# Loads of late weight operands and output weights moved from SyncE's to ScalarE's queue in a gated mix of two linear attentions

## The chip, the cores and the metric

The kernel runs on one core of a Trainium2 chip. A core has five engines with instruction streams of their own: TensorE (PE, matmuls and transposes), VectorE (DVE), ScalarE (ACT), GpSimd (POOL) and SyncE (SP, which here issues transfers only). They wait for each other on semaphores. Transfers (DMAs) are issued by an engine and carried out by 16 DMA engines. The metric is the time of one execution on the device in microseconds (us).

## The reference

Tokens x (2048 x 576) go through two linear attentions of 32 heads with 18 columns each, A and B, whose outputs are mixed by a gate:

```python
def _A_ref(x, wqkv, wo):
    qkv = (lambda x, *d: x.transpose(*d))((x @ wqkv).reshape(B, S, 3, H, Dh), 2, 0, 3, 1, 4)
    q, k, v = qkv[0], qkv[1], qkv[2]
    phi = lambda t: jnp.where(t > 0, t + 1, jnp.exp(t)) + 1e-6
    pq, pk = phi(q), phi(k)
    kv = jnp.einsum("bhsd,bhse->bhde", pk, v)
    z = jnp.einsum("bhsd->bhd", pk)
    num = jnp.einsum("bhqd,bhde->bhqe", pq, kv)
    den = jnp.einsum("bhqd,bhd->bhq", pq, z)[..., None] + 1e-6
    ...  @ wo

def _B_ref(x, wqkv, w_phi, wo):
    ...
    pq = jnp.einsum("bhsd,hdf->bhsf", q, w_phi)
    pk = jnp.einsum("bhsd,hdf->bhsf", k, w_phi)
    phi_q = jnp.concatenate([_softmax(pq, axis=-1), _softmax(-pq, axis=-1)], axis=-1)
    phi_k = jnp.concatenate([_softmax(pk, axis=-1), _softmax(-pk, axis=-1)], axis=-1)
    ...

g = _sigmoid((x * gate_w).sum(-1, keepdims=True))
return g * a + (1 - g) * b
```

## The kernel before

**Tiles and passes.** The 2048 tokens are 16 tiles of 128, worked on in pairs. Every projection is a Strassen product of seven smaller products, whose operands are split in a high and a low part. The weight operands of the seven products lie in `op` tiles (a pool of 11 buffers, 128 x 2304 values each) and `tail` tiles. Three passes follow each other. A's pass makes A's keys and values and adds up A's `kv`; it also forms the x operands and stores them in DRAM (`x0x` to `x3x`, `s0x` to `s2x`). B's pass does the same for B, with the x operands loaded again by `x_fetch`, one pair ahead, into `xu`, `xp`, `x` and `xv`. The query pass computes both queries of a pair, both numerators and denominators, and the output rows.

**Work beside the passes.** In the passes, generators are stepped forward between products. In A's pass `prep_b` and `prep_q1` fold the weights of B. In B's pass `both` (L1003) runs `prep_wo`, then `prep_out` (L918), which multiplies A's `kv` into A's output weight, six column blocks one after the other, in `op` tiles, and stores the rows in DRAM as `MA_d` (named `mad` in the profile); then `prep_q2`, which makes the query weights' operands. At its end `prep_out` copies rows 378 to 570 of `MA_d` into free places of `WO_d` (`wod`), the other half of the output weights, DRAM to DRAM. Of the seven weight operands, four stay in `op` tiles as they are made; operands 7, 4 and 3, the late ones, are written to DRAM (`stage`, the tile `st`, 256 x 1 x 576 in each store; `wb` for B, `wq` for the queries) and come back at the end of the pass by `load_ops` (L619): for B at L914, for the queries at L1033.

**The start of the query pass.** When the query pass begins to run ahead by a pair, `x_fetch` loads the next pair's x operands and `load_out` (L1036) the output weights: four `op` tiles and a tail, three of them from `WO_d` and the rest from `MA_d`, with two small pieces of two rows each. The output matmuls `bk<-op,at` need all of them. The fold of B's `kv` runs there too: ScalarE copies it to `z_b` and `kb`, and PE goes on from there. `late` is a tile that holds queries' features, which PE transposes (`tr<-ident,late`).

**What sets the order.** All engine calls are first recorded as `Op`s of a `Plan`. `weigh` (L201) gives each a cost; that of a DMA is 450 or 740 ns on SP and 60 ns on another engine, with a lag of 5 us. `order` (L234) works back from PE's sequence to the time at which each instruction is due. `run` (L268) then simulates the engines and picks, among those that are ready, the one that is due first; a DMA there goes through one server for all, at 370 bytes a ns. `plan.first` adds a dependence for this planning alone: `load_out`'s loads are planned behind the x loads (`x["dma"]`). `emit` (L343) issues the whole list in the order found, so that in the profile every instruction has line L351. On the chip an engine runs its list in order, and PE too. Semaphores are set for real dependences and for buffers; besides, the DMAs take eight completion semaphores in turn, so that an issue also waits for the landing of the DMA eight issues earlier, whichever engine issued it.

```python
            op.cost = 60 if eng != "SP" else 740 if op.dma < 20000 else 450
            ...
            if op.dma:
                dma = max(s + 1000, dma) + op.dma / 370
                end = dma + 750
```

Of the kernel before, what the change touches and what calls it, by code (L numbers as in the profile page):

```python
# [144 lines left out]
class Plan:  # L145
# [55 lines left out]
    def weigh(self, op, eng, name, out, ins, args, kw):  # L201
        n = max([math.prod(v.shape[1:]) for v in (*ins, out) if isinstance(v, View)])
        psum = any(v.tile.psum for v in (*ins, out) if isinstance(v, View))
        wide = any(v.idx.strides[-1] == 0 for v in ins)
        if name == "dma_start":
            op.dma = math.prod((out if isinstance(out, View) else ins[0]).shape) * 4
            op.cost = 60 if eng != "SP" else 740 if op.dma < 20000 else 450
            op.lag = 5000
        elif eng == "ACT":
            op.cost += 190 + .87 * n  # L210
        elif eng == "POOL":
            tt = name == "tensor_tensor"
            op.cost += (200 + 1.7 * n if wide else 150 + 2.2 * n) if tt else 80 + .85 * n
            op.lock = tt
        elif eng == "DVE":
            fast = name in ("tensor_scalar", "tensor_copy", "memset") and not psum
            op.cost += 120 + 5 * n if name == "reciprocal" else 120 + .6 * n if fast else 80 + 1.04 * n if psum else 75 + 1.03 * n
            op.lag = 85
            op.lock = not psum and name in ("tensor_tensor", "tensor_scalar", "scalar_tensor_tensor")
        else:  # L220
            m = out.shape[0]
            op.lag = self.PE_OUT
            if ins[0].dtype() == F32R and name == "matmul":
                op.cost += 5 + .441 * n if m > 64 else 3 + .221 * n
                op.mode = m <= 64
            elif name == "transpose":
                op.cost += 108
            else:
                n = math.prod(out.shape[1:])
                half = m <= 64 or ins[0].shape[0] <= 64  # L230
                op.cost += 6 + .82 * n if m <= 64 else max(112, 1.75 * n)
                op.mode = half
# [35 lines left out]
    def run(self, tags):  # L268
        ops = self.ops
        for op in ops:  # L270
            op.left, op.est = len(op.deps), 0
        free = {e: 800 for e in ("PE", "ACT", "DVE", "POOL", "SP")}
        ready = {e: [] for e in free}
        slots = {tag: [0] * ts[0].bufs for tag, ts in tags.items()}
        pend = {tag: list(ts) for tag, ts in tags.items()}
        started, last, left = set(), {}, {t: t.ops for ts in tags.values() for t in ts}
        for op in ops:
            if not op.left:
                ready[op.eng].append(op)
        lock, dma, mode = 0, 0, False  # L280
        out = []
        SL = {"PE": 120, "ACT": 250, "DVE": 250, "POOL": 100, "SP": 50}
        while len(out) < len(ops):
            best = None
            for e, ops_e in ready.items():
                cand = []
                for op in ops_e:
                    s = max(free[e], op.est)
                    taken = {}
                    for t in op.tiles:  # L290
                        if t not in started:
                            free_at = sorted(slots[t.tag])
                            k = taken[t.tag] = taken.get(t.tag, -1) + 1
                            if pend[t.tag].index(t) >= len(free_at):
                                s = None
                                break
                            s = max(s, free_at[k])
                    if s is None:
                        continue
                    if op.lock:  # L300
                        s = max(s, lock - (220 if e == "POOL" else 30))
                    cand.append((s, op, 110 if e == "PE" and op.mode != mode else 0))
                if not cand:
                    continue
                first = min(s for s, _, _ in cand)
                due, _, s, op = min((op.due + 2 * turn, op.i, s + turn, op) for s, op, turn in cand if s <= first + SL[e])
                if best is None or s < best[0]:
                    best = (s, e, op)
            s, e, op = best
            ready[e].remove(op)  # L310
            for t in op.tiles:
                if t not in started:
                    started.add(t)
                    pend[t.tag].remove(t)
                    slots[t.tag].remove(min(slots[t.tag]))
            end = s + op.cost
            free[e] = end
            if op.dma:
                dma = max(s + 1000, dma) + op.dma / 370
                end = dma + 750  # L320
            elif e == "PE":
                mode = op.mode
            if op.lock:
                lock = end
            if not op.dma:
                end += op.lag
            op.key = s
            out.append(op)
            for t in op.tiles:
                left[t] -= 1  # L330
                last[t] = max(last.get(t, 0), end + self.SEM)
                if not left[t]:
                    slots[t.tag].append(last[t])
            for i in op.succ:
                o = ops[i]
                o.left -= 1
                o.est = max(o.est, free[e] if o.eng == e and not op.dma else end + self.SEM)
                if not o.left:
                    ready[o.eng].append(o)
        self.span = max(free.values())  # L340
        return out
# [14 lines left out]
def tile_gated_mix(ctx, tc, xT, wAk, wAv, wBv, wAq, wkT, wqT, phi, woA, woB, out):  # L356
# [12 lines left out]
    def r(ap):  # L369
        return ap.bitcast(F32)  # L370
# [248 lines left out]
    def load_ops(W, Wd, x):  # L619
        for op in (7, 4, 3):  # L620
            W[op] = op_tile()
            plan.first = ()
            SP.dma_start(r(W[op]), Wd[op])

    def folds(src, K, ph, raw, ahead):

# [291 lines left out]
    def prep_out():  # L918
# [27 lines left out]
        for c in range(6):  # L946
            wo, nxt = nxt, load(c + 1) if c < 5 else None
            here = [(a, 2 * c + a) for a in range(2 if c < 5 else 1)]
            if c % 2 == 0:
                t = op_tile()  # L950
            k, rows = 2 * (c % 2), 64 * len(here)
            pm = pq_tile()
            with plan.piece():
                for hf in range(2):
                    for a, gr in here:
                        h = slice(64 * a, 64 * a + 54)
                        PE.matmul(pm[64 * a:64 * a + 64, hf, :HB], KA[h, 54 * gr:54 * gr + 64], wo[h, HB * hf:HB * hf + HB],
                                  start=True, stop=True, skip_group_check=True)
            hv, lv = [t[:rows, k + s].rearrange("p (a c) -> p a c", a=2) for s in range(2)]
            A.activation(hv, pm[:rows, :, :HB], AF.Copy)  # L960
            V.tensor_tensor(lv, pm[:rows, :, :HB], r(hv), op=ALU.subtract)
            if c < 4:
                if c % 2:
                    dst = MA_d[108 * (c - 1):108 * (c + 1)].rearrange("(c a q) s n -> a q c s n", c=2, a=2)
                    for a in range(2):
                        SP.dma_start(dst[a], r(t[64 * a:64 * a + 54]).rearrange("p (c s) n -> p c s n", c=2))
            else:
                for a, gr in here:
                    n = min(54, D - 54 * gr)
                    SP.dma_start(MA_d[54 * gr:54 * gr + n], r(t[64 * a:64 * a + n, k:k + 2]))  # L970
            yield
        for a in range(2):
            SP.dma_start(WO_d[64 * a + 54:64 * a + 64, 0:5], MA_d[378:478].rearrange("(k a q) s n -> a q k s n", a=2, q=10)[a])
        SP.dma_start(WO_d[36:, 5], MA_d[478:570])
# [28 lines left out]
    def both():  # L1003
        yield from prep_wo()
        yield from prep_out()
        yield from prep_q2()

    prep = both()
    a_done, pend = pend, []
# [26 lines left out]
    def load_out(x):  # L1036
        for k in range(4):
# [2 lines left out]
            to = r(t).rearrange("p (i s) n -> p i s n", i=2)  # L1040
            plan.first = x["dma"]
            if k < 3:
                SP.dma_start(to, WO_d[:, 2 * k:2 * k + 2])
            else:
                SP.dma_start(to[:126], MA_d[:252].rearrange("(g p) s n -> p g s n", g=2))
                SP.dma_start(to[126:], MA_d[570:574].rearrange("(g p) s n -> p g s n", g=2))
        t = tail_tile()
        WOt.append(t)
        plan.first = x["dma"]
        SP.dma_start(r(t[:126]), MA_d[252:378])  # L1050
        SP.dma_start(r(t[126:]), MA_d[574:])

    WOt = []

# [297 lines left out]
```

## Time and profile before

| what | us |
|---|---|
| median of 3 runs | 574.15 (575.48, 571.35, 574.15) |
| the profiled execution | 575.83 |
| its span on the core | 574.1, at a mean granted PE clock of 0.993 |

The profile is of one execution, taken by the hardware profiler. Its names are those of tiles, out<-in, without buffer numbers: `op<-wod` is the load of an `op` tile from `WO_d`, `pq<-op,xu` a matmul of a weight operand with `xu` into `pq`. SPq and ACTq are the parts of SP and ACT that issue transfers. A matmul of 288 columns is listed with about 297 ns in the groups, but matmuls overlap, so that work on PE is read from one row's start to the next one's. The granted clock is a share of PE's full speed. The DMA share is the busy share of the 16 DMA engines. The late operands for B leave SP from 124.33 on, at the end of A's pass, and those for the queries up to 276.83, at the end of B's; the start of the query pass is what happens from 300 to 340.

### The profile page before, as it was taken

The numbers are of one execution on the slowest core, as the hardware profiler recorded it, in microseconds if no ns is written. First come the engines' busy times: TensorE is split into PE (matmuls) and PEld (weight loads), VectorE is DVE, ScalarE is ACT, GpSimd is POOL, SyncE is SP. The second block draws the span as 40 slices with busy tenths as digits, with TensorE's granted clock in tenths as the row PEclk, the third lists the DMA queues.
The fourth block names the chain that finished last, engine by engine and source line by source line (L and its number), as shares of the span: only waits on it lengthen the run. The fifth ranks groups of instructions, "written<-read, shape, count | busy, mean of one in ns | idle before, by whom it ended". The sixth has DMA issues, their size and how long they took to land.

```text
span 574.1 us, 11726 instructions
## 1 busy us (share of the span) xinstructions
PE 555.1 (97%) x4584; PEld 529.5 (92%) x4584; DVE 422.8 (74%) x665; ACT 286.4 (50%) x602; POOL 252.4 (44%) x226
## 2 busy tenths in 40 slices
PE   8999999999999998999899799999999999999997
PEld 8999999999999888999898789898998989999897
DVE  7773479723799877999879878959679595987910
ACT  6766687556644433443345455345354354435431
POOL 5683798642954312543228645124242241523200
PEclk9999999999999999999999799999999999999999
DMA  8768567999795666667949522132232313200011
GB/s 305 253 212 280 182 244 274 319 322 385 259 396 169 201 209 209 210 216 217 384 126 324 214 84 74 41 117 72 77 94 67 104 66 104 76 2 22 22 42 41
DMA packets 40209, 100.73 MB, mean 175 GB/s; under 512 B 4282, under 2 KB 7610, under 8 KB 38618
## 3 DMA queue, kind: packets, MB, share of 16 engines
q1 hardware_dynamic: 40154, 99.99, 50.7%
q8 instruction: 36, 0.59, 0.4%
q14 instruction: 19, 0.16, 0.1%
HBM read 64.15 MB, written 36.70 MB: 176 GB/s over the span
## 4 chain that ended last, share of the span: by engine, by line
PE 73%; DVE 11%; DMA 8%; POOL 3%; issue 2%; ACT 2%; SPq 1%; POOLq 0%; ACTq 0%; DVEq 0%
PE pq L351 30%; PE bk L351 23%; PE tr L351 19%; DMA xu<-x0x 3%; DVE row L351 2%; DVE at L351 2%; DMA x<-x3x 2%; DVE ss L351 1%; DMA wq<-st 1%; DMA wb<-st 1%; DVE mm L351 1%; DMA uw<-wqT 1%; DVE vo L351 1%; DVE dd L351 1%; DVE uw L351 1%
## 5 line engine op out<-in xcount | busy, mean ns | idle before, releaser
L351 PE MATMUL pq<-op,x 128*128 128x288 f32 (+1 forms) x636 | 102.4, 297 | 0.0
L351 PEld LDWEIGHTS pq<-op,x 128*128 128x128 f32 x636 | 90.1, 188 | 0.7 <-issue 0.4
L351 PE MATMUL bk<-op,vo 128*128 128x288 f32 x480 | 71.0, 297 | 0.0
L351 PE MATMUL pq<-tail,x 128*128 128x288 f32 (+1 forms) x308 | 66.7, 300 | 2.0 <-DMA x<-x3x 2.0
L351 PEld LDWEIGHTS bk<-op,vo 128*128 128x128 f32 x480 | 65.8, 188 | 0.2 <-DVE vo L351 0.2
L351 PE MATMUL pq<-op,xp 128*128 128x288 f32 (+1 forms) x336 | 54.2, 298 | 0.0
L351 PEld LDWEIGHTS pq<-tail,x 128*128 128x128 f32 x308 | 49.0, 188 | 3.4 <-issue 2.9
L351 PE MATMUL bk<-op,at 128*128 128x288 f32 x288 | 52.1, 305 | 0.0
L351 POOL TENSOR_TENSOR row<-row,z_a 128x576 f32<-128x576 f32 x16 | 22.7, 1420 | 65.3 <-issue 35.6
L351 PEld LDWEIGHTS pq<-op,xp 128*128 128x128 f32 x336 | 47.7, 188 | 0.2
L351 ACT ACTIVATE row<-bk 128x288 f32<-128x288 f32 x38 | 15.6, 410 | 64.3 <-PE bk L351 64.3
L351 ACT ACTIVATE row<-row,epsc 128x576 f32<-128x576 f32 x54 | 41.9, 776 | 10.1 <-DVE row L351 9.0
L351 DVE TENSOR_TENSOR row<-row,pq 128x576 f32<-128x576 f32 (+1 forms) x30 | 22.5, 751 | 32.0 <-ACT row L351 16.0
L351 POOL TENSOR_TENSOR row<-row,den 128x378 f32<-128x378 f32 (+1 forms) x32 | 24.6, 787 | 48.5 <-DVE den L351 40.0
L351 ACT ACTIVATE row<-tr 128x288 f32<-128x288 f32 (+1 forms) x74 | 29.8, 407 | 30.0 <-PE tr L351 29.6
L351 DVE TENSOR_REDUCE ss<-uw 128x64 f32<-128x1152 f32 x23 | 30.9, 1349 | 16.8 <-ACT uw L351 16.1
L351 PEld LDWEIGHTS bk<-op,at 128*128 128x128 f32 x288 | 42.5, 192 | 0.4 <-issue 0.4
L351 ACT ACTIVATE uw<-uw 128x1152 f32<-128x1152 f32 x23 | 26.7, 1165 | 28.5 <-DVE uw L351 18.7
L351 POOL TENSOR_TENSOR x<-at,x 128x384 fp32r<-128x384 f32 (+2 forms) x36 | 31.3, 877 | 21.0 <-ACT x L351 11.9
L351 DVE TENSOR_TENSOR at<-at 128x256 f32<-128x256 f32 (+1 forms) x40 | 31.2, 817 | 7.4 <-DMA at<-xT 7.0
L351 ACT ACTIVATE uT<-tr 118x512 f32<-118x512 f32 (+1 forms) x48 | 25.9, 559 | 20.9 <-PE tr L351 20.8
L351 PE MATMUL tr<-op,xv 128*128 128x288 f32 (+1 forms) x204 | 34.0, 303 | 0.0
(184 smaller groups left out, 1264.6 us busy)
## 6 DMA issues: line engine op xcount, KB each, us to landing
xp<-s0x SPq DMA_DIRECT2D x14, 512.0 KB
at<-xT SPq DMA_DIRECT2D x20, 320.0 KB
x<-x1x SPq DMA_DIRECT2D x14, 384.0 KB
x<-s2x SPq DMA_DIRECT2D x14, 384.0 KB
s0x<-xp SPq DMA_DIRECT2D x8, 512.0 KB
out<-row SPq DMA_DIRECT2D x14, 288.0 KB
xu<-x0x SPq DMA_DIRECT2D x14, 256.0 KB
x<-s1x SPq DMA_DIRECT2D x14, 256.0 KB
```

Source lines behind the costliest of these rows:

```text
L351: fn(*[a.real() if isinstance(a, View) else a for a in args], **{k: v.real() if isinstance(v, View) else v for k, v in kw.items()})
```

## The change

Three things are edited. `load_ops` and `load_out` issue their loads on ScalarE (`A.dma_start`) instead of SP, 13 DMAs in all. The copies from `MA_d` into `WO_d` leave `prep_out` for a new generator, `join_out`, which `both` runs after `prep_q2`, that is, at the end of B's pass as the code is written. And the planner changes its model: a DMA on another engine than SP costs 350 ns instead of 60, and there is a server of transfers for each of the two queues, at 370 bytes a ns or 185 while the other is busy.

```diff
-            op.cost = 60 if eng != "SP" else 740 if op.dma < 20000 else 450
+            op.cost = 350 if eng != "SP" else 740 if op.dma < 20000 else 450
@@ run
-        lock, dma, mode = 0, 0, False
+        lock, dma, mode = 0, {"SP": 0, "ACT": 0}, False
@@
-                dma = max(s + 1000, dma) + op.dma / 370
-                end = dma + 750
+                dma[e] = max(s + 1000, dma[e]) + op.dma / (370 if max(dma.values()) <= s + 1000 or dma[e] > s + 1000 else 185)
+                end = dma[e] + 750
@@ load_ops
             W[op] = op_tile()
-            plan.first = ()
-            SP.dma_start(r(W[op]), Wd[op])
+            A.dma_start(r(W[op]), Wd[op])
@@ prep_out
             yield
+
+    def join_out():
         for a in range(2):
             SP.dma_start(WO_d[64 * a + 54:64 * a + 64, 0:5], MA_d[378:478].rearrange("(k a q) s n -> a q k s n", a=2, q=10)[a])
         SP.dma_start(WO_d[36:, 5], MA_d[478:570])
@@ both
         yield from prep_q2()
+        yield from join_out()
@@ load_out
             if k < 3:
-                SP.dma_start(to, WO_d[:, 2 * k:2 * k + 2])
+                A.dma_start(to, WO_d[:, 2 * k:2 * k + 2])
             else:
-                SP.dma_start(to[:126], MA_d[:252].rearrange("(g p) s n -> p g s n", g=2))
-                SP.dma_start(to[126:], MA_d[570:574].rearrange("(g p) s n -> p g s n", g=2))
+                A.dma_start(to[:126], MA_d[:252].rearrange("(g p) s n -> p g s n", g=2))
+                A.dma_start(to[126:], MA_d[570:574].rearrange("(g p) s n -> p g s n", g=2))
...
-        SP.dma_start(r(t[:126]), MA_d[252:378])
-        SP.dma_start(r(t[126:]), MA_d[574:])
+        A.dma_start(r(t[:126]), MA_d[252:378])
+        A.dma_start(r(t[126:]), MA_d[574:])
```

Since the planner lays out the whole program, the order of the engines' lists changes where due times and costs changed. SP's list in the middle of B's pass, where A's output rows are stored (`mad<-op`) and copied (`wod<-mad`) between the loads of the next pair's x operands:

```order
-L351 DMA x_2690<-s1x_991 128x512
+L351 DMA x_2691<-s1x_991 128x512
 L351 DMA wod<-mad 10x5x1152 x2
+L351 DMA mad<-op 36x1152
 L351 DMA xv<-x2x_1023 128x512
-L351 DMA x_2729<-x3x_1060 128x256
-L351 DMA mad<-op 36x1152
-L351 DMA x_2769<-s2x_1077 128x768
+L351 DMA x_2732<-x3x_1060 128x256
+L351 DMA x_2770<-s2x_1077 128x768
 L351 DMA wod<-mad 92x1152
```

The copies stand in the same places in both. The last store of A's rows, 36x1152, moved ahead of the loads of `xv` and x3x.

SP's list at the end of B's pass, with the late query operands (`op<-wq`) and the store of the last of them (`wq<-st`):

```order
 L351 DMA xu<-x0x_155 128x512
-L351 DMA op<-wq_2875 128x2304
-L351 DMA wq_3111<-st 256x1x576
-L351 DMA op<-wq_2980 128x2304
 L351 DMA x_3399<-x1x_165 128x768
-L351 DMA xp<-s0x_1841 128x1024
-L351 DMA op<-wq_3111 128x2304
-L351 DMA x_3479<-s1x_1853 128x512
+L351 DMA xp<-s0x_1820 128x1024
+L351 DMA x_3479<-s1x_1864 128x512
```

The three loads are gone from SP, and the store stands further up in its list.

ScalarE's list at the start of the query pass, where it copies B's folded `kv` from PSUM (`z_b<-bk`, `kb<-bk`):

```order
 L351 ACTIVATE z_b<-bk 128x3x2x54 x2
+L351 DMA op<-mad 126x2x1152
 L351 ACTIVATE z_b<-bk 128x2x2x54 x2
 L351 ACTIVATE z_b<-bk 128x2x36
+L351 DMA tail<-mad 126x1152
+L351 DMA op<-wod 128x2304
 L351 ACTIVATE kb<-bk 108x8x54
 L351 ACTIVATE kb<-bk 108x2x54
 L351 ACTIVATE kb<-bk 72x36
```

Three of the seven loads of the output weights now stand between these copies; the other four come behind them.

PE's list at the same place (`x_3660` is an x operand of the pair in work, `xu` one of the next pair):

```order
 L351 MATMUL bk<-op,xp 128x288 x12
-L351 MATMUL bk<-op,x_3660 128x288 x9
-L351 MATMUL tr<-ident,late 118x128 x8
-L351 MATMUL bk<-op,x_3660 128x288 x3
-L351 MATMUL bk<-op,xv 128x288 x2
+L351 MATMUL bk<-op,x_3660 128x288 x6
+L351 MATMUL pq<-op,xu 128x288
+L351 MATMUL bk<-op,x_3660 128x288 x2
+L351 MATMUL tr<-ident,late 118x128 x8
```

The first matmul on `xu` moved up, ahead of work that stood before it.

PE's list a little further on, where the first output matmuls (`bk<-op,at`, `bk<-tail,at`) stand; `x_3746` is an x operand of the pair in work:

```order
-L351 MATMUL pq<-op,xu 128x288 x12
-L351 MATMUL bk<-op,at 128x288 x6
-L351 MATMUL bk<-tail,at 128x288 x3
-L351 MATMUL pq<-op,x_3746 128x288 x2
-L351 MATMUL tr<-ident,late 118x128 x8
-L351 MATMUL pq<-op,x_3746 128x288 x4
...
+L351 MATMUL pq<-op,xu 128x288 x11
+L351 MATMUL tr<-ident,late 118x128 x8
+L351 MATMUL bk<-op,at 128x288 x6
+L351 MATMUL bk<-tail,at 128x288 x2
```

Eight transposes moved ahead of the output matmuls, and six matmuls on `x_3746` moved behind this place.

## The prediction, on record before the run

> **What bounds the kernel now.** I read the page first: which engine is full, and what ends the chain.
>
> ```profile
> PE 555.1 (97%) x4584; PEld 529.5 (92%) x4584; DVE 422.8 (74%) x665; ACT 286.4 (50%) x602; POOL 252.4 (44%) x226
> PEclk9999999999999999999999799999999999999999
> q1 hardware_dynamic: 40154, 99.99, 50.7%
> PE 73%; DVE 11%; DMA 8%; POOL 3%; issue 2%; ACT 2%; SPq 1%; POOLq 0%; ACTq 0%; DVEq 0%
> ```
>
> TensorE (PE) is busy 97% of the span, so the matmuls set the time and a change of the transfers can win only PE's idle time and the time lost at a low clock. The clock is below full in one slice of 40 only. All data goes through one queue, q1. The chain of work that ended last has 8% of the span in transfers. Next, therefore, PE's waits by what ended them (total us, times, longest):
>
> ```profile
> PE pq L351 <- DMA xu<-x0x: 3.9, 1, 3.9
> PE tr L351 <- ACT uw L351: 2.3, 1, 2.3
> PE pq L351 <- DMA x<-x3x: 2.0, 1, 2.0
> PE pq L351 <- DMA uw<-wqT: 0.9, 1, 0.9
> ```
>
> These are single waits. In PE's timeline (start, busy time, idle time and releaser in brackets) they stand at three places that the change touches, A's last output rows (219.7), the end of B's pass (287.1) and the start of the query pass (322.0):
>
> ```profile
> 219.70 1.87 PE L351 MATMUL tr<-op,xp 128*128 128x288 f32 x12 [2.34 <-ACT uw L351]
> 287.09 0.50 PE L351 MATMUL pq<-tail,x 128*128 128x288 f32 x2 [1.97 <-DMA x<-x3x]
> 309.56 1.36 PE L351 MATMUL bk<-op,x 128*128 128x288 f32 x9
> 317.72 0.42 PE L351 MATMUL pq<-tail,x 128*128 128x288 f32 x2
> 322.04 3.25 PE L351 MATMUL pq<-op,xu 128*128 128x288 f32 x12 [3.89 <-DMA xu<-x0x]
> 325.08 1.65 PE L351 MATMUL bk<-op,at 128*128 128x288 f32 x6
> 327.24 0.43 PE L351 MATMUL pq<-op,x 128*128 128x288 f32 x2
> 327.51 1.03 PE L351 MATMUL tr<-ident,late 128*118 128x128 f32 x8
> 329.51 0.95 PE L351 MATMUL pq<-op,x 128*128 128x288 f32 x6
> 333.50 0.82 PE L351 MATMUL pq<-op,xp 128*128 128x288 f32 x5
> 365.54 0.96 PE L351 MATMUL bk<-op,at 128*128 128x288 f32 x6
> ```
>
> What each cost in clock is in the table by stretch (from:to, length, busy of PE, weight load, VectorE (DVE), ScalarE (ACT) and GpSimd (POOL), clock, DMA share, GB/s):
>
> ```profile
> 124.00:128.00 4.00, 3.08 (x25) 2.87 (x24) 0.76 (x1) 1.28 (x3) 1.61 (x2) 1.00 1.06 407
> 217.00:220.00 3.00, 0.66 (x5) 0.42 (x4) 0.62 (x1) 2.33 (x4) 1.42 (x1) 1.00 0.40 135
> 284.00:288.00 4.00, 2.03 (x16) 1.82 (x15) 3.83 (x6) 0.82 (x2) 0.13 (x1) 1.00 0.75 259
> 304.00:322.00 18.00, 12.99 (x93) 11.66 (x93) 17.38 (x30) 11.14 (x28) 15.25 (x16) 0.96 1.00 333
> 322.00:326.00 4.00, 3.96 (x16) 3.96 (x17) 4.00 (x7) 0.00 (x0) 3.24 (x4) 0.50 0.41 141
> 326.00:328.00 2.00, 2.00 (x14) 2.00 (x13) 1.90 (x5) 0.00 (x0) 0.82 (x2) 0.69 0.40 131
> ```
>
> The waits of 2.34 and 1.97 left the clock at 1.00. That of 3.89 was followed by 0.50 for four microseconds and 0.69 for two: 4 x 0.50 + 2 x 0.31 = 2.6 us of full-clock work lost. The start of the query pass so loses 3.9 + 2.6 = 6.5 us, of which the transfers are the cause, at a DMA share of 1.00 from 304 to 322. The chain gives the transfers themselves (start, time to landing):
>
> ```profile
> 214.55 2.99 DMA mad<-op
> 278.19 8.76 DMA x<-x3x
> 307.09 14.90 DMA xu<-x0x
> 121.82 5.35 DMA uw<-wqT
> 251.68 3.61 DMA wq<-st
> ```
>
> and the list of transfers their sizes, by the number of such transfers and KB of each:
>
> ```profile
> op<-wq SPq DMA_DIRECT2D x3, 1152.0 KB
> x<-x3x SPq DMA_DIRECT2D x14, 128.0 KB
> xu<-x0x SPq DMA_DIRECT2D x14, 256.0 KB
> ```
>
> **The change part by part.** The sum is made against the profiled execution, 575.83 us, which is 1.68 above the median of 574.15.
>
> *A's last output rows.* The words say that the copies into WO_d move to the end of B's pass; the order shows them where they were, so that part costs and brings nothing (both ends zero, unless a queue moves around them). What moves is the last store of A's rows, ahead of two x loads.
>
> ```profile
> 212.83 1.67 SPq L351 DMA_DIRECT2D x<-x3x  x1
> 276.83 0.32 SPq L351 DMA_DIRECT2D op<-wq  x1
> 300.24 0.42 SPq L351 DMA_DIRECT2D op<-mad  x1
> 302.35 1.32 SPq L351 DMA_DIRECT2D op<-wod  x3
> 217.61 0.68 ACT L351 ACTIVATE op<-row 128x576 fp32r<-128x576 f32 x1 [7.35 <-DMA mad<-op]
> 301.53 0.75 ACT L351 ACTIVATE z_b<-bk 128x324 f32<-128x324 f32 x2
> 304.62 0.76 ACT L351 ACTIVATE kb<-bk 108x432 f32<-108x432 f32 x3 [0.62 <-PE bk L351]
> ```
>
> The store was issued at 214.55 and landed 2.99 later, 217.54, and ScalarE, which had waited 7.35 for the buffer that the store reads, went on at 217.61; PE then waited 2.34 for ScalarE's next result. Issued ahead of the x loads it goes out at 212.3 at the earliest, so ScalarE is freed up to 2.2 us sooner. If the store shares the engines with the copies issued at 210.57 it gains about 1. I take the middle, **-1.6** (-1.0 to -2.2). Next late there is VectorE, 0.62 busy of 3 us, so nothing takes the wait's place.
>
> *Late weight operands.* Of the six loads the three of B's pass are issued by ScalarE near 125, where it is 1.28 us busy of 4; they wait there for the landing of earlier transfers, and what is queued behind them on ScalarE is wanted by nobody for microseconds: 0. The third load at the end of B's pass went out at 276.83 on SP, 1152 KB, and x<-x3x behind it took 8.76 us for 128 KB and landed at 286.95, when PE had waited since 285.1. It now leaves from ScalarE, and earlier, since the store that it reads moved ahead too. By the nearest row of a transfer that is not held up, 3.61 for wq<-st, x3x lands at 281.8, 3.3 us before it is asked for. The wait of 1.97 can go whole; but VectorE is 3.83 busy of 4 there, so part can come back as a wait for it: **-1.7** (0 to -2.0).
>
> *Output weights.* The seven loads fill the engines from 304 on, and xu, issued at 307.09 behind all of them in one queue, landed at 321.99. As the queue takes them in order, the output weights were in by then too. Three things happen to them now.
>
> First, ScalarE issues them after its second z_b, at 301.53 + 0.75 = 302.3, 2.0 us after SP did (300.24). Second, xu no longer stands behind them. It still cannot be issued before 307.09, which a matmul's end sets. When it lands the trace does not show: 2.99 is the shortest such transfer in the chain, 14.90 what it took in one queue; I take 5.35, that of uw<-wqT, which ran into saturated engines (share 1.06 in 124 to 128): 307.09 + 5.35 = 312.4. Third, PE's first matmul on xu moves ahead of other work. It comes after six of the nine matmuls of the row at 309.56, so at 309.56 + 0.9 = 310.5, where before PE had 318.14 - 310.5 = 7.65 us of work left ahead of it. PE waits 312.4 - 310.5 = 1.9, less than the 2.34 that left the clock alone. Then come the 7.65 us, to 320.1, the remaining matmuls on xu at full clock, 3.25 / 2 = 1.6, and the eight transposes that now stand ahead of the output matmul, 0.8 of the 1.03: 322.5.
>
> There PE asks for all output weights, bk<-op,at. They end 2.0 us later than at 322.0 for the late start, and later by xu's 256 KB, which at 333 GB/s is 0.7: 324.7 (322 if the start costs nothing, 326.4 if the x loads behind xu pass as well). PE waits 2.2. After it: 0.96 for the six (the full-clock row at 365.54), 0.5 for the tail, 1.1 for what is left up to the row at 329.51, about half of the 2.3 us between 327.24 and there, since the eight transposes are gone from it (six matmuls on x_3746 now stand further back, but PE still has to do them): 327.3. Before it was 329.5: **-2.2** (-6.5 if neither wait appears). That both waits stay under the 2.34 is my choice; should the clock fall, the 2.2 is gone.
>
> By the Trainium skill, DMA: Bandwidth & Descriptors, "Queues, rings and completion order", an engine alternates between the queues that have work, packet by packet; the 256 KB would then go at half of 333 GB/s, an estimate of 1.5 us, xu would land little after 308.6, and the first wait would go, 1.9 more than in the sum above. No row here shows two queues at work.
>
> *ScalarE's price.* SP's rows give 0.3 to 0.44 us for one issue. Two of the seven stand ahead of kb<-bk, at 304.62, which PE waits for; ScalarE had 0.62 us free there, so 2 x 0.44 - 0.62 = **+0.3** (0.1 to 1.0). SP's later x loads still wait for the same transfers to land, but the first, xp, comes to PE only at 333.50.
>
> Sum: -1.6 - 1.7 - 2.2 + 0.3 = **-5.2**: 570.6 on the profiled execution, 569.0 as a median.
>
> **The rivals.** *Slower: xu gets no faster, and PE asks for it sooner.* Both queues end on the same 16 engines, full at 1.00 from 304 to 322, with 333 GB/s for all. If packets are served about in the order of issue, xu still takes 14.9, and now 7.65 us of PE work that ran before it stand behind it: +7.7 at the query start, with the clock as low as before, and 7.7 - 1.6 - 1.7 + 0.3 = +4.7: median 578.9. It decides from a landing 10.2 us after the issue on (322.0 - 4.7 - 307.1). For it: the order of PE did move, and one queue is all the trace shows. Against it: uw<-wqT took 5.35 under a full load, though in the same queue.
>
> *The stall only changes its name.* The bytes are the same, and what PE waits for at 322 becomes the output weights, later by their start and with the clock down again: the third term is 0, 575.83 - 3.0 = 572.8, median 571.1. For it: 333 GB/s through the whole stretch, and DVE at 17.38 of 18. The Trainium skill, DMA: Bandwidth & Descriptors, "Issuing engines are not separate DMA queues", speaks for it: transfers share the same 16 engines whoever starts them, and a second issuer saves issue time alone. The share of 1.00 agrees.
>
> *All of it goes.* xu lands before 310.5, the weights by 322.5: -2.2 - 2.0 - 6.5 + 0.1 = -10.6, median 563.5. Against it: the later start of the weights.
>
> **How the numbers follow.** Forecast 0.45 (own range 566.5 to 571.5), the changed name 0.2, slower 0.2 (574 to 584), all of it 0.15. About 1%, 5.7 us, is what a measurement of this kernel can tell from no change. Faster than 568.4: four tenths of the forecast (0.18), all of it (0.15), a little of the changed name (0.03), 0.36. Slower than 579.9: a little under half of the slower case and 0.03 for what I haven't seen, 0.12. The range 563.5 to 578 leaves out half of each end case.
>
> **What would show it.** Right: two queues with data; ScalarE's op<-row near 216 and no 2.34 behind it; no wait for x3x at 285; xu landing some 5 us after its issue, and PE waiting for op<-wod or op<-mad near 322 with the clock at 1.00. Wrong: xu at 10 us or more after its issue with a PE wait near 311 and a clock of 0.50 behind it; a wait for kb of over 1 us near 305; or the copies to WO_d standing elsewhere than now.

## The result, and the profile after

The changed kernel takes 581.78 us as a median of 6 runs (579.95 to 587.91), against 574.82 for the kernel before on the same chips (6 runs, 571.35 to 581.13): 1.0132 times as long, with a 95% interval of 1.0092 to 1.0171. It is slower, where the prediction was 569.0 with a range of 563.5 to 578. The profiled execution took 579.95 us, with a span of 578.2 against 574.1.

PE's waits and the queues in the profile after, from the table of waits (total us, times, longest) and the page:

```profile
PE pq L351 <- DMA xu<-x0x: 5.6, 1, 5.6
PE pq L351 <- DMA uw<-wqT: 4.5, 2, 3.9
...
PE tr L351 <- ACT uw L351: 1.3, 1, 1.3
```

```profile
q1 hardware_dynamic: 38442, 87.60, 44.4%
q10 hardware_dynamic: 1712, 12.39, 5.6%
```

The wait for x3x is gone and that for ScalarE's `uw` is down from 2.3 to 1.3. But xu now costs 5.6 instead of 3.9, and the `uw<-wqT` loads at the end of A's pass (pieces of B's query weight, 320 KB or less), 0.9 before, cost 4.5. The 13 loads do run in a queue of their own, q10. PE's timeline after, at the two places that lost:

```profile
126.86 1.35 PE L351 MATMUL pq<-at,uw 126*128 126x126 f32 x10 [0.64 <-DMA uw<-wqT]
...
135.87 2.01 PE L351 MATMUL pq<-at,uw 126*128 126x126 f32 x10 [3.88 <-DMA uw<-wqT]
...
318.34 0.58 PE L351 MATMUL pq<-op,xu 128*128 128x288 f32 x1 [5.60 <-DMA xu<-x0x]
...
327.91 1.62 PE L351 MATMUL pq<-op,xu 128*128 128x288 f32 x11
...
330.17 1.04 PE L351 MATMUL bk<-op,at 128*128 128x288 f32 x6
```

`bk<-op,at` has no wait in brackets: the output weights, which the prediction made the second wait, were in. The chain of work after gives the two transfers (start, time to landing), and the table by stretch what the clock did behind them (the eighth number is the clock):

```profile
124.09 11.65 DMA uw<-wqT
...
309.26 8.94 DMA xu<-x0x
```

```profile
132.00:136.00 4.00, 0.13 (x1) 0.16 (x2) 0.68 (x1) 0.72 (x2) 1.26 (x1) 1.00 1.05 359
136.00:140.00 4.00, 4.00 (x21) 4.00 (x22) 0.00 (x0) 1.17 (x3) 0.00 (x0) 0.57 0.99 383
...
318.00:322.00 4.00, 3.66 (x16) 3.67 (x17) 0.00 (x0) 1.19 (x2) 0.23 (x1) 0.50 0.90 372
322.00:326.00 4.00, 4.00 (x26) 3.95 (x25) 2.26 (x6) 3.32 (x8) 1.48 (x2) 0.74 0.19 66
```

Both long waits were followed by a clock of about a half.

All kernels of this case have the same 4584 matmuls on PE, so one can read how far a run lags behind another by comparing the starts of the matmul with the same number. The table takes four stretches, named by the time in the profile of before, and gives how much each profiled execution gained or lost in it against that of before:

| us lost (+) or won (-) | end of A's pass (129.9 to 153.5) | A's last rows (214.8 to 226.2) | end of B's pass (261.1 to 298.9) | query start (298.9 to 346.0) | at the last matmuls |
|---|---|---|---|---|---|
| the changed kernel | +4.9 | -1.1 | -2.2 | +2.2 | +4.1 |
| e1, before's order, 13 loads on ScalarE | +7.5 | +1.8 | +1.7 | -3.6 | +7.6 |
| e2, the new order, 13 loads on SP | +5.4 | -1.2 | -2.2 | +7.0 | +9.7 |
| e3, late operands only | +4.4 | -1.4 | -2.2 | -1.1 | -0.4 |
| e4, output weights only | -0.2 | +3.5 | -1.6 | +1.3 | +3.5 |
| e5, before's order, output weights on ScalarE | 0.0 | +2.4 | -2.0 | -0.7 | -0.5 |
| e6, e5 and the queries' operands | +0.3 | +2.6 | +4.5 | -4.5 | +1.5 |
| e9, one server, B's operands on SP | -0.1 | +2.4 | +2.5 | -5.4 | +1.3 |
| e10, before's order, B's operands on ScalarE | +6.1 | +4.3 | -1.8 | +0.1 | +9.3 |
| e11, one server, output weights on ScalarE | +0.5 | +1.7 | -2.0 | -5.1 | -5.4 |
| e12, e11 and the last store on ScalarE | 0.0 | -2.6 | -2.0 | -5.1 | -9.0 |
| e13, the change, B's operands on SP | -0.2 | +3.5 | +2.7 | +0.7 | +6.3 |

What is left of a row's sum came up at other places. The table shows the noise too: e4, e5, e10 and e11 have before's lists on every engine at A's last rows, and lost 1.7 to 4.3 us there against the one execution of before that was profiled; and with the third `op<-wq` still on SP they won 1.6 to 2.0 at the end of B's pass. So that execution of before was lucky at the first place, by some 2 to 4 us, and unlucky at the second, by about 2.

### The profile page after: what moved, and what is told of

It reads as the page before. It is cut to its first block, busy times and chain, and to the rows that moved or that the text cites. A ratio compares the mean times of both kernels' runs of the same rounds, so it can differ in the third digit from the quotient of the medians.

```text
span 578.2 us, 11728 instructions
## 1 busy us (share of the span) xinstructions
PE 557.1 (96%) x4584; PEld 531.6 (92%) x4584; DVE 419.7 (73%) x665; ACT 287.8 (50%) x602; POOL 252.7 (44%) x226
## 4 chain that ended last, share of the span: by engine, by line
PE 78%; DVE 11%; DMA 6%; POOL 2%; issue 1%; ACT 1%; POOLq 0%; ACTq 0%; DVEq 0%
PE pq L351 33%; PE tr L351 23%; PE bk L351 22%; DMA uw<-wqT 2%; DVE row L351 2%; DMA wq<-st 2%; DVE ss L351 2%; DVE den L351 2%; DMA xu<-x0x 2%; DVE dd L351 1%; DVE mm L351 1%; DVE rs L351 1%; DVE uw L351 1%; DMA x<-x3x 1%; POOL late L351 1%
## 5 line engine op out<-in xcount | busy, mean ns | idle before, releaser
L351 DVE TENSOR_TENSOR vo<-row,pq 128x540 f32<-128x540 f32 (+1 forms) x56 | 22.8, 449 | 17.9 <-ACT row L351 15.0
```

The costliest lines, as they stand in the source:

```text
L351: fn(*[a.real() if isinstance(a, View) else a for a in args], **{k: v.real() if isinstance(v, View) else v for k, v in kw.items()})
```

## The experiments

The first four take the change apart in two ways: order and queue, and the two groups of loads.

**e1: before's order, the 13 loads issued by ScalarE.** They are recorded as SP's for the planner, so that every list stands as before, and issued by ScalarE:

```diff
+    QA = Engine(plan, "SP", nc.scalar)
@@ load_ops
-            SP.dma_start(r(W[op]), Wd[op])
+            QA.dma_start(r(W[op]), Wd[op])
@@ load_out, all loads
-                SP.dma_start(to, WO_d[:, 2 * k:2 * k + 2])
+                QA.dma_start(to, WO_d[:, 2 * k:2 * k + 2])
```

> Before's planned order on every engine, kept; the 13 loads are issued by ScalarE at the places in time where SP issued them. Theory O (the order): the loss of the changed kernel comes from PE's list, which asks for uw (near 132) and xu (near 312.7) 3 and 6 us sooner than two queues deliver. Then here uw is in when PE asks at 135.3 (wait under 1 us), xu lands about 9 us after its issue at 307, before PE asks at 318.1, the 6.5 us of the query start go, and the kernel is 4 to 7 us faster than before: 567 to 571. Theory Q (the queue): the loads in a second queue take the DMA engines from SP's small loads, which come late whatever the order. Then uw takes over 11 us and PE waits 1 to 2.5 us at 135, with xu landing no sooner than 318, and the time is 574 to 580.

Measured: 583.03 us, 1.0135 times before (1.0051 to 1.0219). Theory O holds at the query start, where no wait for xu is left and 3.6 us are won; theory Q holds at the end of A's pass:

```profile
142.24 2.47 PE L351 MATMUL pq<-at,uw 126*128 126x126 f32 x10 [5.75 <-DMA uw<-wqT]
```

PE asked for this `uw` no sooner than before, and still waited 5.75 us: it took 15.68 from its issue at 126.42. So neither theory is right alone (the time lies outside the ranges of both), and my expectation put one name on two places that differ.

**e2: the new order, the 13 loads on SP.** The reverse: recorded as ScalarE's, issued by SP (`QS = Engine(plan, "ACT", nc.sync)` in `load_ops` and `load_out`).

> The changed kernel's planned order, kept; the 13 loads are issued by SP again, at the places in time where ScalarE issued them. Theory O: PE still asks for uw near 132 and for xu near 312.7; xu stands behind the output weights and takes about 14.9 us again, so PE waits about 11 us there: 583 to 590. Theory Q: without a second queue uw is in by 132 to 133, the 4.5 us of that stage come back, and only xu is late: 575 to 580.

Measured: 585.65 us, 1.0176 (1.0101 to 1.0250), as theory O has it.

```profile
132.66 1.28 PE L351 MATMUL pq<-at,uw 126*128 126x126 f32 x10
139.89 1.92 PE L351 MATMUL pq<-at,uw 72*128 72x72 f32 x10 [3.00 <-DMA uw<-wqT]
```

```profile
324.74 0.58 PE L351 MATMUL pq<-op,xu 128*128 128x288 f32 x1 [11.11 <-DMA xu<-x0x]
```

In one queue the second `uw`, which PE waits for after the change, is in by 132.66, so theory Q is right about it; but the third is now asked for too soon, and the stage costs 5.4 us all the same. At the query start xu took 14.41 us again and the wait was 11.11.

PE's list at the end of A's pass shows what the prediction passed over (before with -, the change with +):

```
+L351 MATMUL pq<-at,uw 128x126 x5
 L351 MATMUL tr<-op,x_1603 128x290 x12
 L351 MATMUL bk<-row,vo 55x54 x10
...
-L351 MATMUL pq<-at,uw 128x126 x5
+L351 MATMUL pq<-at,uw 128x72 x5
 L351 MATMUL tr<-op,xv 128x290 x6
 L351 MATMUL tr<-tail,x_1670 128x290 x2
-L351 MATMUL tr<-op,xv 128x290 x5
-L351 MATMUL pq<-at,uw 128x72 x5
```

Here too matmuls on a loaded operand moved ahead of 12 transposes and of the `kv` matmuls, some 3 us of work.

**e3 and e4: one group of loads each.** e3 leaves `load_out` on SP, e4 leaves `load_ops` on SP (with its `plan.first = ()`); the rest is the change, planned anew.

> The change with the output weights' loads left on SP, planned anew. Both theories put a loss of about 4.5 us near uw (131 to 142), a gain of about 1 at A's last output rows and of about 2 at x3x, and the query start as before: 1 to 2 us over before, 575 to 577. If the loss of the changed kernel were all in the query start, this one would be 3 us faster than before, 571.

> The change with the late weight operands' loads left on SP, planned anew. Until 300 us as before. Both theories: xu lands about 9 us after its issue, PE, asking for it near 310.5, waits about 5.6 us with the clock falling to half behind it, and the query start costs about 2 us more than before: 575.5 to 578. If xu's landing depended on the earlier queue changes, its wait would differ from 5.6 us by over 1.

Measured: e3 577.72 us, 1.0036 (1.0000 to 1.0072); e4 578.31 us, 1.0058 (1.0018 to 1.0098), both a little above the times expected. e3 has the loss at the end of A's pass, +4.4, and e4 has the wait for xu:

```profile
318.36 0.58 PE L351 MATMUL pq<-op,xu 128*128 128x288 f32 x1 [5.63 <-DMA xu<-x0x]
```

It landed 8.93 us after its issue, as in the changed kernel (8.94), so the earlier stages don't matter to it. The two groups' losses come at different places, and each comes without the other group.

**e5: before's order, only the output weights on ScalarE.**

> Before's planned order on every engine; only the seven loads of the output weights are issued by ScalarE. Theory O (what costs at the query start is PE's new order, what gains there is the queue): xu lands about 9 us after its issue, before PE asks for it, no PE wait of over 1 us and no lower clock from 304 to 330, and the kernel is 5 to 7 us faster than before: 568 to 571 against some 575. Theory N (the gain seen there with both loads moved came from PE running 13 us behind): xu still makes PE wait 2 us or more, and the time is within 2 us of before.

Measured: 573.24 us, 0.9981 (0.9939 to 1.0023): no difference that shows. xu no longer stops PE, but the next thing does:

```profile
323.90 1.03 PE L351 MATMUL bk<-op,at 128*128 128x288 f32 x6 [2.63 <-DMA op<-mad]
```

```profile
320.00:324.00 4.00, 1.37 (x11) 1.17 (x10) 3.84 (x8) 2.18 (x5) 3.92 (x5) 1.00 0.87 342
324.00:328.00 4.00, 4.00 (x21) 3.98 (x22) 3.91 (x8) 0.81 (x2) 3.53 (x4) 0.61 0.53 157
```

That is the rival of the prediction in which the stall only changes its name. Theory O was right about xu and wrong about the time: with before's order the output weights are asked for too early.

**e6: e5, and the queries' late operands planned and issued on ScalarE.**

> As the run with before's order and only the output weights on ScalarE, and the queries' late operands (end of B's pass) planned and issued on ScalarE too; B's stay on SP. If x3x waited for the third of these loads in one queue, its 2 us go as well: 7 to 9 us faster than before, 566 to 568. If ScalarE pays for the issues by waiting for earlier transfers, as it did with before's order kept and all 13 loads on it (3.8 us lost from 261 to 284), the gain at x3x is given back: 570 or more.

Measured: 576.68 us, 1.0034 (0.9997 to 1.0071). The gain at the query start, 4.5, is lost at the end of B's pass. ScalarE's timeline (idle time and its releaser in brackets):

```profile
280.64 0.33 ACTq L351 DMA_DIRECT2D op<-wq  x1
281.02 0.71 ACT L351 ACTIVATE row<-tr 128x288 f32<-128x288 f32 x2 [9.64 <-DMA wq<-st]
```

The third `op<-wq` has to wait until its data is stored, `wq<-st`; on SP only transfers queued behind it, on ScalarE it held the activations for 9.64 us, and PE 4.6 of them.

**e9: one server of transfers in the planner, B's operands on SP.** The new model is taken back, and the rest of the change is left, but for B's operands:

```diff
-        lock, dma, mode = 0, {"SP": 0, "ACT": 0}, False
+        lock, dma, mode = 0, 0, False
@@
-                dma[e] = max(s + 1000, dma[e]) + op.dma / (370 if max(dma.values()) <= s + 1000 or dma[e] > s + 1000 else 185)
-                end = dma[e] + 750
+                dma = max(s + 1000, dma) + op.dma / 370
+                end = dma + 750
```

> The changed kernel, but the planner has one server of transfers for both queues again (370 bytes a ns in all), and B's late operands stay on SP. PE's list then asks for xu behind more work than before. Theory O: no wait for xu, no wait for uw beyond before's 0.9, 7 to 9 us faster than before: 566 to 568. If PE's order isn't what costs, it is no faster than the changed kernel less its loss at uw: 577.

Measured: 575.49 us, 1.0012 (0.9981 to 1.0043), a miss by 7 us or more. At the query start PE waits neither for xu nor for the output weights and 5.4 us are won, as theory O has it. In the profile 2.5 us went where e6 lost them, at the end of B's pass, where ScalarE waited 5.07 us for `wq<-st`, 2.4 at A's last rows and 2.7 ahead of 129.9.

**e10: before's order, only B's three late operands on ScalarE.**

> Before's planned order on every engine; only B's three late operands (end of A's pass) are issued by ScalarE. Theory S (a second queue slows the small loads of the first while 3.4 MB run beside them): the second uw takes over 12 us from its issue and PE waits 3 to 6 us for it near 136, with the clock down behind it: 4 to 7 us slower than before. Theory B (with all 13 loads moved it was ScalarE that was held up by waiting to issue): uw in time, PE waits for ScalarE instead.

Measured: 582.86 us, 1.0152 (1.0082 to 1.0223), some 8 us slower and so more than the 4 to 7 expected. Theory S:

```profile
126.44 15.32 DMA uw<-wqT
```

```profile
141.90 2.47 PE L351 MATMUL pq<-at,uw 126*128 126x126 f32 x10 [5.03 <-DMA uw<-wqT]
```

At this place PE waits for no activation, which rules out theory B. With the lists of before, the second `uw` took 15.32 us with the three loads in the other queue; in before itself it was issued at 125.72 and in by 135.31, 9.6 at most.

**e11: the output weights on ScalarE, all late operands on SP, one server in the planner.** e9 with all of `load_ops` as before.

> Only the output weights on ScalarE, all late operands on SP, and the planner with one server of transfers for both queues. It differs from the run with the output weights alone on ScalarE in the planner's model only: there PE asked for xu at 312.7 and waited 5.6 us. Theory O (the planner's two servers promise data that the shared engines don't bring): PE's list is laid out for the real rate, no wait for xu or for output weights of over 0.5 us, the clock stays at 1.00 from 304 to 332, and some 6 us go: ratio to before 0.988 to 0.992. Against it: if it is within 0.5% of before, the query start's 6 us are given back elsewhere.

Measured: 570.91 us, 0.9931 (0.9903 to 0.9959): faster, by less than the 0.988 to 0.992 expected. It differs from e4 only in the planner's model (and what that makes of the order), and the query start goes from +1.3 to -5.1. No wait for xu or the output weights is left, and the clock stands at 1.00 where before had 0.96, 0.50 and 0.69:

```profile
304.00:322.00 18.00, 16.70 (x122) 15.11 (x121) 16.92 (x30) 12.41 (x31) 15.76 (x15) 1.00 0.98 365
322.00:326.00 4.00, 4.00 (x34) 2.84 (x32) 3.97 (x9) 1.74 (x3) 4.00 (x5) 1.00 0.48 153
326.00:328.00 2.00, 2.00 (x16) 1.84 (x15) 1.93 (x5) 1.53 (x6) 0.94 (x2) 1.00 0.00 0
```

PE is busy 16.70 of the 18 us, 12.99 before. This order with the loads left on SP was not run, so what the second queue adds to it stays open.

**e12: e11, and the last store of A's rows issued by ScalarE.**

```diff
-                    SP.dma_start(MA_d[54 * gr:54 * gr + n], r(t[64 * a:64 * a + n, k:k + 2]))
+                    (A if c == 5 else SP).dma_start(MA_d[54 * gr:54 * gr + n], r(t[64 * a:64 * a + n, k:k + 2]))
```

> As the run with the output weights on ScalarE and one server, and the last store of A's output rows is issued by ScalarE as soon as it is ready. If that store's place on SP behind two x loads is what holds ScalarE (and PE, 2.3 to 4.4 us, in every run so far with the old place), the wait falls under 1.5 us as in the changed kernel and 1 to 4 us go on top: ratio to before 0.982 to 0.990. If the store itself is slow, the wait stays and the ratio is that of the other run.

Measured: 566.59 us (565.60 to 567.97), 0.9857 (0.9813 to 0.9901), the fastest of all, and faster than both kernels. ScalarE's timeline:

```profile
211.25 0.55 ACTq L351 DMA_DIRECT2D mad<-op  x1
214.72 0.69 ACT L351 ACTIVATE op<-row 128x576 fp32r<-128x576 f32 x1 [2.46 <-DMA mad<-op]
```

The store goes out at 211.25 (214.14 in e11, 214.55 in before), and the activation that needs its buffer waits 2.46 us (7.60 and 7.35). PE's wait there is gone, and 4.3 us with it (e11 lost 1.7 at this place, e12 won 2.6).

**e13: the change with B's operands back on SP.**

> The changed kernel with B's late operands back on SP, the rest as changed (planner with two servers, queries' operands and output weights on ScalarE). If the loss near 134 comes from these three loads, it goes: PE's wait for uw falls from 4.5 to about 1 us and the stage is as before, 5 us better than the changed kernel. But the stores wq<-st are then as late as before, ScalarE waits for one of them before the third op<-wq, 5 to 10 us, and PE loses 3 to 6 us near 284 in the place of the 2.2 that the changed kernel gained there. Sum: 577 to 582, no better than the changed kernel by more than 4.

Measured: 582.37 us, 1.0128 (1.0074 to 1.0183). The loss at the end of A's pass is gone (-0.2), but as foreseen another takes its place: ScalarE waited 8.56 us for `wq<-st`, and the end of B's pass lost 2.7 where the change had won 2.2; A's last rows are as slow as in the other runs with the old place of the store.

With `join_out`, the new cost and the two servers, but all loads on SP, the planner makes the very lists of before on every engine, so the move of the copies by itself changes no list. That kernel was not run.

## Why the prediction was wrong

**The step that failed first** is the price of B's late operands: "they wait there for the landing of earlier transfers, and what is queued behind them on ScalarE is wanted by nobody for microseconds: 0". I asked who waits behind the moved loads on ScalarE, and not who is left beside them on SP. The stage costs +4.9 us: 3.88 of waiting for the second `uw` and a clock of 0.57 behind it. Two things meet. In before's one queue the second `uw` stood behind one `op<-wb` and ahead of the next; with the loads in a second queue it took 11.65 (15.32 in e10, 15.68 in e1) instead of at most 9.6. And PE's list asks for it some 3 us earlier. Each alone costs the stage as much, 6.1 (e10, queue) and 5.4 (e2, order); together 4.9. The stage had no slack to give: PE already waited 0.92 for the first of these loads, in a row that I had quoted.

**The query start** was given as -2.2 and was +2.2. Of its steps, that PE asks for xu earlier was right (312.7, at a program 2.2 us late, so 310.5 of before's clock). Mis-sized was the landing, 8.94 us after the issue instead of 5.35: the wait was 5.6 instead of 1.9, long enough for the clock to fall (0.50, then 0.74). The second wait that the sum had, 2.2 for the output weights, didn't come, since PE asked for them only at 330.17; in e5, where it asked at 321.27, it did wait, 2.63. What I called the slower rival was this mechanism; its landing "about in the order of issue" was wrong, as two queues do bring xu sooner (8.94 against 14.41 in e2 with the same order), but not as much sooner as the planner moved the matmul. Its break-even of 10.2 us was that of the whole kernel, with 3.0 us of other gains in it. For the query start alone its sum gives 14.9 - 7.7 = 7.2 us, and so a loss of 1.7 at 8.94, near the 2.2 measured. With the other gains that would still have been a kernel 1.3 us faster; that the measured time lies within the rival's 574 to 584 is luck, since the 4.9 us at the end of A's pass were in no sum of the prediction.

**What made the two landings late** is in the trace of the changed kernel, by queue (packets, MB, share of the engines' time). From xu's issue at 309.26 to 313.5 only q10 moved data:

```profile
q10 hardware_dynamic: 206, 1.37, 101.6%
```

From 313.5 to xu's landing at 318.2:

```profile
q10 hardware_dynamic: 187, 1.50, 77.1%
q1 hardware_dynamic: 186, 0.43, 23.5%
```

From 128.0 to 135.74, the landing of the second `uw`:

```profile
q10 hardware_dynamic: 274, 2.32, 78.2%
q1 hardware_dynamic: 301, 0.68, 24.0%
```

So xu's first packet came 4.2 us after the issue; a load of the same 256 KB, issued at 322.10 when q10 was done, had its first after 0.9. Why it took so long is open. After that the queues got about as many packets each, but a packet of the output weights or of `op<-wb` in q10 holds some 8 KB and one in q1 some 2.3 on average, so that q1 was left with a quarter of the engines' time and not with half.

**A's last rows**: the mechanism was right, -1.6 given and -1.1 in the two profiles. Against the eight runs with the old place of the store (+1.7 to +4.3) it is more, and e12 shows 4.3.

**x3x**: -1.7 given, -2.2 in the profile, but little of it by the change: e4, e5, e10 and e11, with the load still on SP, won 1.6 to 2.0 there too. A wait of 2.0 in one execution was taken for a property of the kernel.

**That the copies stay where they were** was right, and so was **ScalarE's price** in its size: `kb` costs PE 0.4 as before, and the stretch from 298.9 up to it is 0.3 longer. (The prediction counted two loads ahead of `kb`; the order shows three.) What e6, e9 and e13 lose, an issue on ScalarE that waits for its own data, does not happen in the changed kernel, since with B's loads off SP the stores `wq<-st` leave early enough (e3 shows it without the output weights).

**The sum of the profile** is +4.9 - 1.1 - 2.2 + 2.2 and small change, +4.1; the medians differ by 7.0. The rest is the choice of executions: the profiled one of the changed kernel, the fastest of its six, lies 1.8 below its median, and that of before 1.0 above its own. What an execution at the median loses more, and where, no trace shows.

**The Trainium skill**, DMA: Bandwidth & Descriptors, has two sections that the prediction weighed. "Issuing engines are not separate DMA queues" says that a second issuer saves issue time alone; here it changed the landing of single transfers by 5 us and more, both ways, so the measurement decides against it as a rule for one transfer, while the bytes as a whole went no faster (433 and 434 GB/s from 128 to 132 in e2 and e1). "Queues, rings and completion order" lets an engine alternate between queues packet by packet, and the packets of the two queues agree (187 and 186); the estimate of 1.5 us for xu that the prediction drew from it was off by 7, as 8.94 shows, since it gave xu half of the bytes and no time ahead of its first packet.

## What to carry to other kernels

A queue that is served in order is also a list of priorities: a second queue lets a small transfer pass the bulk, and takes that away from the small transfers which stood ahead of the bulk. So count, for each transfer that stays in the old queue, how much slack it has when most of the engines' time goes to the new one (here 77 and 78%, since its packets were larger). When a planner lays out the order, its model of the transfers must not promise more than the shared engines bring, since a matmul that it moves up to a load that is still late holds up all work behind it, and this costs more than the wait itself once the clock falls: the same loads on the same queues were 0.6% slower with two servers in the model and 0.7% faster with one. And a DMA goes to a computing engine only if its data is ready when it gets there.

## What the runs showed of the hardware that was not expected

The clock fell after shorter waits than the one that the prediction took as harmless. In before a wait of 2.34 left it at 1.00; in e9 one of 2.25, at the end of B's pass, was followed by 0.62, in e11 one of 2.51, at A's last rows, by 0.73, and in e5 one of 2.63 by 0.61. So between 2.2 and 2.4 us the length of a wait alone does not decide. The rows of e9, then of e11, in the table of waits and in the table by stretch:

```profile
PE tr L351 <- ACT row L351: 2.3, 1, 2.3
```

```profile
292.00:296.00 4.00, 4.00 (x22) 4.00 (x21) 3.83 (x6) 0.41 (x1) 0.00 (x0) 0.62 0.02 4
```

```profile
PE tr L351 <- ACT uw L351: 2.5, 1, 2.5
```

```profile
220.00:224.00 4.00, 3.34 (x18) 3.34 (x19) 3.52 (x5) 1.91 (x6) 2.23 (x2) 0.73 0.63 202
```

Two queues moved no more than one: from 128 to 132 it was 434 GB/s in e1, with two, and 433 in e2, with one, at DMA shares of 1.06 and 1.07. What the second queue changed is which transfer was served when: packet for packet in turn, and so by the size of the packets.
